# Reordering the hand-over from the first to the second batch of a fused attention and feed-forward kernel

## The chip, the cores and the metric

The kernel runs on one core of a Trainium2 chip. Its time is the device time of one execution in microseconds (us). Engines are called by the names of the profile: PE is TensorE (PEld its weight loads), ACT ScalarE, DVE VectorE, POOL GpSimd, SP SyncE.

## What is computed

```python
# q, k, v: (8, 12, 448, 64) float32: batches, heads, sequence, head size
scores = q @ k.T / sqrt(64) - log(448)
attn   = 1 / (1 + exp(-scores))                 # a sigmoid, no softmax
x      = (attn @ v) -> (8 * 448, 768)           # heads side by side
out    = (max(x @ w_gate, 0) * (x @ w_val)) @ w_out   # 768 -> 1536 -> 768
```

## The kernel before, in words

**Tiles.** A batch has twelve heads, taken in three groups of four (`NG`). The 448 positions of a sequence lie as 64 rows times seven chunks (`NCH`). For scores, keys and queries have to stand with the head dimension on the partitions: a tile `qkT` of a group holds seven chunks of transposed keys and seven of transposed queries. There are three such tiles in turn. Batches 0 and 1 are transposed on TensorE (`pe_transposes`, L195 to L209: up to 14 transposes into one PSUM bank, then one VectorE copy, L206). From batch 2 on, VectorE copies keys and queries into a tile `rel` (L215) and a DMA transpose on the SP queue writes `qkT` (L219).

**Scores and attention.** A score unit (`qk_unit`, L292) is one chunk of keys against all queries of its group: 4 matmuls of 64x64 weights that run side by side, two PSUM banks, and two sigmoid activations of 128x448 on ScalarE (L187). `pv` (L242) sums attention times values over the seven chunks in 28 matmuls and two banks; VectorE scales the sums into `xT` (L184).

**Feed-forward.** `gv` (L304) is one chunk of 128 of the 1536 hidden columns: six matmuls for the gate, six for the value (L309), then max(gate, 0) on ScalarE (L318; on VectorE, L320, for the chunks of batch 0 that are queued with `False`), and the product on VectorE (L327). The chunks stand in `gv_queue`, and `ffn_mix(n)` (L659) takes the next n of it; its hooks are pairs (left, job), and a job is done as soon as no more than `left` chunks are left to do. The projection back to 768 columns follows from batch 2 on, with sums of the weights made by VectorE (`weight_sums`, L403 with L384).

**Batch 0** is handled apart (`FirstSlot`, L263). Its queries are cut in two halves, 256 and 192 columns, so that work can begin with part of them: slots 0 to 2 are the groups with the first half, slots 3 to 5 with the second, each of four score units into two double banks (`pairp`). The table `after` (L691) says what is done behind which unit: transposes, matmuls that keep the clock up, `pv`, and chunks of the feed-forward, which have 256 or 192 columns in this batch.

**Batch 1 and later** (loop at L789). The 21 score units of a batch are cut into six bursts (`cuts`). Behind each burst come `mix[m]` chunks of the batch before; `pv_at` says where within a burst a group's `pv` goes. For batch 1 the hooks put the transposes of groups 1 and 2 (`both`) and the DMA transposes of batch 2 between these chunks.

**Loads.** All loads from L132 on are issued by GpSimd in the order of the program, and convert float32 to float16 on the way. `hold` (L734) is a tiny GpSimd copy out of a `qkT` tile: it keeps GpSimd from issuing the next load before that tile's DMA transpose has landed.

**PSUM** has eight banks. Four are the ring from the start, the other four are batch 0's double banks and join the ring when it is done (L731); each product takes the next bank of the ring.

Of the kernel before, what the change touches and what calls it, by code (L numbers as in the profile page):

```python
# [17 lines left out]
def kernel(  # L18
# [17 lines left out]
    NCH = S // 64  # L36
# [3 lines left out]
    QCUT = 4  # L40
# [40 lines left out]
    def bank16(name):  # L81
        return bank(name, (P, 1024), FP16)
# [20 lines left out]
    def rows_of(src, b):  # L103
        return src[b].rearrange("(x r) (t c) d -> (r t) x (c d)", r=2, c=NCH)

    def load(b, g0, g1, which, c0=0, c1=NCH):
        for nm, t16, src in zip("kq", tiles_of(b), (k, q)):
            if nm in which:
                xs, cs = slice(2 * g0, 2 * g1), slice(c0 * D, c1 * D)
                nc.gpsimd.dma_start(t16[:, xs, cs], rows_of(src, b)[:, xs, cs])  # L110
# [10 lines left out]
    KCUT = 4  # L121
# [22 lines left out]
    def load_gv(f0, f1, which=(0, 1)):  # L144
        fs = slice(f0 * P, f1 * P)
        for i in which:
            wt, src = ((wg, moe_w_gate), (wv, moe_w_val))[i]
            nc.gpsimd.dma_start(wt[:, :, fs], src[:, fs].rearrange("(c p) f -> p c f", p=P))
# [2 lines left out]
    load(0, 1, NG, "q", QCUT)  # L151
    load_gv(0, 2, (1,))
    load_gv(2, 4)
    load_gv(4, 6)
    load(1, 0, 1, "kq")
    load_gv(6, 9)
    load(1, 1, 2, "kq")
    load_v(1)
# [36 lines left out]
    def pe_transposes(b, g, ti, c0=0, c1=NCH):  # L195
        t16 = in_tiles[b][ti]
        qkT = qkT_of(b, g)
        trt = bank16("trt")
        for c in range(c0, c1):
            for h in range(2):  # L200
                nc.tensor.transpose(  # L201
                    trt[64 * h : 64 * h + 64, c * P : (c + 1) * P],
                    t16[:, 2 * g + h, c * D : (c + 1) * D],
                    ident[:],
                )
        nc.vector.tensor_copy(  # L206
            qkT[:, ti * NCH + c0 : ti * NCH + c1, :].rearrange("p c x -> p (c x)"),
            trt[:, c0 * P : c1 * P],
        )  # L209

    def dma_transposes(b, g):
        k16, q16, _ = in_tiles[b]
        rel = relp.tile([P, TW, P], FP16, tag="rel", name="rel")
        for ti, t16 in enumerate((k16, q16)):
            nc.vector.tensor_copy(  # L215
                rel[:, ti * NCH : (ti + 1) * NCH, :].rearrange("p c (h d) -> p h c d", h=2),
                t16[:, 2 * g : 2 * g + 2, :].rearrange("p h (c d) -> p h c d", c=NCH),
            )
        nc.sync.dma_start_transpose(  # L219
            qkT_of(b, g)[:], rel[:].rearrange("p c x -> p (c x)")  # L220
        )
# [433 lines left out]
    def push_first(half, fs, act_relu=True):  # L655
        c0, c1 = HALVES[half]
        push_gv(0, 64 * c0, 64 * (c1 - c0), fs, act_relu)

    def ffn_mix(count, hooks=()):  # L659
        hooks = list(hooks)  # L660
        for left in range(count, -1, -1):
            while hooks and hooks[0][0] >= left:
                hooks.pop(0)[1]()
            if left:
                gv_queue.popleft()()
# [8 lines left out]
    pe_transposes(0, 0, 1, 0, QCUT)  # L674
    keep_warm(2)
    slots = [FirstSlot(half * NG + g, g, half) for half in range(2) for g in range(NG)]
    push_first(0, range(0, 6), False)
    def second_queries():
        for g in range(1, NG):
            pe_transposes(0, g, 1, QCUT, NCH)  # L680

    def pv_then_ffn(i):
        slots[i].pv()
        ffn_mix(1)

    def ffn_then_pv(i):
        ffn_mix(1)
# [3 lines left out]
    after = {  # L691
        (0, 0): lambda: pe_transposes(0, 0, 0, KCUT, NCH),
        (0, 1): lambda: keep_warm(2),
        (0, 2): lambda: pe_transposes(0, 1, 0),
        (0, 3): lambda: pe_transposes(0, 1, 1, 0, QCUT),
        (1, 0): lambda: keep_warm(2),
        (1, 1): lambda: pe_transposes(0, 2, 0),
        (1, 2): lambda: pe_transposes(0, 2, 1, 0, QCUT),
# [7 lines left out]
        (3, 3): lambda: ffn_mix(1),  # L706
        (4, 1): lambda: ffn_then_pv(3),
        (4, 3): lambda: ffn_mix(2),
        (5, 1): lambda: pv_then_ffn(4),
        (5, 3): lambda: ffn_mix(1),  # L710
    }
    for i, slot in enumerate(slots):
        for u in range(4):
# [1 line left out]
            if (i, u) in after:  # L715
                after[(i, u)]()
    slots[5].pv()
    push_first(1, range(0, 6))
    for f0 in range(6, 12, 2):
        for half in range(2):  # L720
            push_first(half, range(f0, f0 + 2))

# [11 lines left out]
    def hold(b, g):  # L734
        nc.gpsimd.tensor_copy(gate[0:1, :], qkT_tiles[(b, g)][0:1, 0, 0:2])

    def both(b, g):
        pe_transposes(b, g, 0)
        pe_transposes(b, g, 1)

    def late_loads():
        dma_transposes(2, 2)
        hold(2, 1)
        load_o()


# [38 lines left out]
            prepare()  # L785
            down(g, i)

    ffn_mix(1, [(1, lambda: both(1, 0))])
    for b in range(1, B):  # L789
        if b == 1:  # L790
            cuts, pv_at = (0, 3, 6, 9, 13, 17, 21), {3: (0, 2), 5: (1, 2)}
        else:
            cuts, pv_at = (0, 4, 7, 11, 14, 18, 21), {0: (-1, 2), 2: (0, 2), 4: (1, 2)}
        bursts = list(range(len(cuts) - 1))
        inner = {}
        if b > 2:
            inner = {0: 1} if b % 2 == 0 else {2: 3, 3: 5} if b == B - 1 else {4: 5}
            for n in inner.values():
                bursts.remove(n)
        count = len(bursts)  # L800
        hooks = {}
        if b == 1:
            mix = (3, 3, 3, 3, 3, 2)
            hooks = {
                1: [(1, lambda: both(1, 1))],
                3: [(1, lambda: both(1, 2))],
                4: [(3, lambda: dma_transposes(2, 0))],
                5: [(2, lambda: dma_transposes(2, 1)), (0, late_loads)],
            }
        elif b == 2:  # L810
            mix = (2, 2, 1, 1, 1, 2)
            hooks = {
                2: [(0, prepare)],
                4: [(0, lambda: weight_sums(0))],
                5: [(1, lambda: weight_sums(1)), (0, lambda: weight_sums(2))],
            }
            open_late()
        elif b == 3:
            mix = (1, 1, 1, 0, 0)
        else:  # L820
            mix = (0,) * count

        def burst(n):
            for i, (g, c) in enumerate(order[cuts[n] : cuts[n + 1]]):
                if n in pv_at and i == pv_at[n][1]:
                    if n == 0:
                        pv_finish(b - 1)
                        if b == 2:
                            push_group(0)
                        elif b % 2 == 0:  # L830
                            push_group(b // 2 - 1)
                    else:
                        pv_group(b, pv_at[n][0])
                qk_unit(b, g, c)

        if b == 3:
            dma_transposes(3, 2)
            for args in put_off:
                stored(*args)
        for m in range(count):  # L840
            jobs = []
            burst(bursts[m])
            if m == 0 and b > 3:
                jobs.append(lambda: dma_transposes(b, 2))
            if b == 2 and m == count - 1:
                jobs.append(lambda: (dma_transposes(3, 0), dma_transposes(3, 1)))
            elif b == 3 and m == count - 1:
                jobs.append(lambda: dma_transposes(4, 1))
            elif 0 <= m - count + 2 and 3 < b < B - 1:
                jobs.append(lambda: dma_transposes(b + 1, m - count + 2))  # L850
            if b == 1:
                if m == 0:
                    load(2, 0, 1, "kq")
                    load(2, 1, 2, "kq")
                    load(2, 2, 3, "kq")
                    load_v(2)
            elif m == 0 and b + 1 < B:
                if b == 3:
                    jobs.append(lambda: hold(3, 2))
                jobs.append(lambda: (load(b + 1, 0, 3, "kq"), load_v(b + 1)))  # L860
            if b % 2 and b > 2:
                if m == count - 1:
                    jobs.append(lambda: (batch_sums_t1(b // 2), batch_sums(b // 2, (0, 1))))
            elif b > 3 and m == 0:
                jobs.append(lambda: batch_sums(b // 2 - 1, (1, HD)))
            if b == 2 and m == count - 1:
                ffn_mix(mix[m], hooks[m])
                next_work(jobs + [lambda: weight_sums(3)], first_act=True)
            elif mix[m]:
                for job in jobs:  # L870
                    job()
                ffn_mix(mix[m], hooks.get(m, ()))
            else:
                next_work(jobs, amid=(lambda: burst(inner[m])) if m in inner else None)
            if b == 3 and m == count - 2:
                dma_transposes(4, 0)
            if b == 3 and m in (1, 3):
                for f in range(*((0, 8, 2), (8, NFC, 2))[m // 2]):
                    gate_sums(f, f + 2)
# [35 lines left out]
```

## Time and profile before

| | us |
|---|---|
| median of 3 runs (lowest, highest) | 392.95 (392.91, 393.34) |
| the profiled execution | 392.75 |
| its span, from first to last instruction | 391.0 |
| PE busy | 384.2 |
| DVE busy | 283.5 |
| ACT busy | 226.9 |

In the lists that follow, a row of a timeline gives the start within the span, how long the row lasts, engine, line, operation, the tile written and those read, the shape and the number of instructions, and in brackets the engine's idle time before it with what ended that. A row of the waits gives who waited for what, the total, how often and the longest. A row of the DMA issues ends with the time from issue to landing. In the row of 40 slices a 9 stands for 90% or more; one slice is 9.8 us. The chain of waits (the work that ended last, in order of time) gives each stretch of matmuls its time up to the next.

### The profile page before, as it was taken

How to read it: one execution, taken by the hardware profiler on the slowest of the kernel's cores; microseconds unless marked ns; L12 is line 12 of the kernel's file. 1: busy time of each engine (PE TensorE's matmuls, PEld its weight loads, DVE VectorE, ACT ScalarE, POOL GpSimd, SP SyncE). 2: the span in 40 equal slices, each digit the busy share in tenths (PEclk: the TensorE clock that was granted, in tenths of full speed). 3: DMA queues.
4: the chain of work that ended last, by engine and by line, in shares of the span. 5: the costliest groups of instructions: out<-in, count | busy, mean ns of one | idle time of the engine just before them, and what ended most of it. 6: DMA issues, size and time to landing. Idle time of an engine off the chain costs nothing.

```text
span 391.0 us, 8760 instructions
## 1 busy us (share of the span) xinstructions
PE 384.2 (98%) x3488; PEld 214.8 (55%) x3488; DVE 283.5 (73%) x557; ACT 226.9 (58%) x480; POOL 49.5 (13%) x73
## 2 busy tenths in 40 slices
PE   8999999999999999999999999999999999999996
PEld 3678786445455545454555554545455555555663
DVE  2454344358387789999757789999987788999663
ACT  5946778784777755555556774545467354333322
POOL 8633420500300300003000300000000000000000
PEclk9999999999999999999999999999999999999999
DMA  9999999998999892225956595132002320000335
GB/s 149 197 199 204 204 204 138 145 202 148 191 185 167 156 217 44 47 49 64 179 99 137 114 222 86 21 49 59 18 14 73 78 80 2 0 1 2 78 87 159
DMA packets 68953, 43.69 MB, mean 112 GB/s; under 512 B 35888, under 2 KB 65584, under 8 KB 68912
## 3 DMA queue, kind: packets, MB, share of 16 engines
q0 software_dynamic: 30736, 23.33, 39.8%
q1 hardware_dynamic: 37664, 19.24, 24.3%
q10 hardware_dynamic: 512, 0.56, 0.5%
q8 instruction: 27, 0.44, 0.5%
q14 instruction: 14, 0.11, 0.1%
HBM read 47.19 MB, written 11.01 MB: 149 GB/s over the span
## 4 chain that ended last, share of the span: by engine, by line
PE 90%; DMA 5%; POOL 1%; DVE 1%; ACT 1%; issue 0%; POOLq 0%; DVEq 0%; ACTq 0%
PE u L393 33%; PE g L393 16%; PE y L393 10%; PE qk_ps L232 8%; PE pv_ps L250 7%; PE g_ps L309 7%; PE v_ps L309 6%; DMA wv<-in_moe_w_val_dram 4%; DMA v<-in_v_dram 2%; PE ya L354 1%; PE trt L201 1%; PE yb L354 1%; POOL k L110 1%; POOL q L110 1%; ACT PT L187 1%
## 5 line engine op out<-in xcount | busy, mean ns | idle before, releaser
L187 ACT ACTIVATE PT<-qk_ps 128x448 f16<-128x448 f32 (+3 forms) x318 | 150.8, 585 | 76.2 <-PE qk_ps L232 76.1
L393 PEld LDWEIGHTS <-S 128*128 128x128 f16 x558 | 54.6, 98 | 44.7
L605 DVE TENSOR_TENSOR gsb<-g,gsb 128x448 f32<-128x448 f32 x72 | 42.8, 625 | 10.3 <-PE g L393 10.0
L232 PE MATMUL qk_ps<-qkT 64*64 64x448 f16 (+2 forms) x756 | 47.4, 335 | 0.8 <-DVE qkT L206 0.5
L327 DVE TENSOR_TENSOR hT<-gate_sb,v_ps 128x256 f16<-128x256 f32 (+2 forms) x36 | 16.2, 465 | 35.2 <-ACT gate_sb L318 18.0
L393 PEld LDWEIGHTS <-hT 128*128 128x128 f16 x306 | 28.7, 98 | 22.3 <-issue 4.9
L601 ACT COPY gsb<-u 128x448 f32<-128x448 f32 x48 | 25.6, 558 | 24.0 <-PE u L393 22.9
L445 ACT ACTIVATE ysb<-u 128x384 f32<-128x384 f32 x31 | 15.2, 491 | 38.2 <-PE u L393 33.8
L250 PE MATMUL pv_ps<-PT,v 64*64 64x448 f16 (+2 forms) x756 | 36.6, 329 | 0.0
L184 DVE TENSOR_SCALAR xT<-pv_ps 128x448 f16<-128x448 f32 (+2 forms) x53 | 27.9, 567 | 11.9 <-PE pv_ps L250 10.8
L309 PE MATMUL v_ps<-xT,wv 128*128 128x256 f16 (+2 forms) x216 | 33.3, 290 | 0.4 <-DMA wv<-in_moe_w_val_dram 0.4
L309 PE MATMUL g_ps<-xT,wg 128*128 128x256 f16 (+2 forms) x216 | 33.5, 291 | 0.1
L393 PEld LDWEIGHTS <-wg 128*128 128x128 f16 x216 | 20.2, 98 | 21.8 <-issue 4.3
L393 PEld LDWEIGHTS <-wv 128*128 128x128 f16 x216 | 21.1, 98 | 19.7
L232 PEld LDWEIGHTS <-qkT 64*64 64x64 f16 x756 | 17.9, 105 | 22.0 <-issue 14.7
L463 DVE SCALAR_TENSOR_TENSOR ysb<-y,ysb 128x384 f32<-128x384 f32 x29 | 16.1, 556 | 17.9 <-PE y L393 10.4
L250 PEld LDWEIGHTS <-v 64*64 64x64 f16 x756 | 21.7, 107 | 10.8 <-issue 0.9
L393 PE MATMUL u<-T,hT 128*128 128x384 f16 x132 | 25.1, 326 | 0.0
L110 POOL DMA_DIRECT2D k<-in_k_dram x14 | 10.9, 776 | 112.4 <-DVE rel L215 105.7
L309 PEld LDWEIGHTS <-wg 128*128 128x128 f16 x216 | 18.5, 98 | 11.7 <-issue 5.1
L309 PEld LDWEIGHTS <-wv 128*128 128x128 f16 x216 | 20.1, 98 | 8.1 <-DMA wv<-in_moe_w_val_dram 0.7
L393 PE MATMUL u<-xT,wg 128*128 128x448 f16 x108 | 23.5, 354 | 0.0
(76 smaller groups left out, 531.2 us busy)
## 6 DMA issues: line engine op xcount, KB each, us to landing
out_dram<-ysb SPq DMA_DIRECT2D x52, 192.0 KB, 2.8
k<-in_k_dram POOLq DMA_DIRECT2D x5, 672.0 KB, 11.4
q<-in_q_dram POOLq DMA_DIRECT2D x5, 672.0 KB, 14.7
v<-in_v_dram POOLq DMA_DIRECT2D x8, 336.0 KB, 14.9
v<-in_v_dram POOLq DMA_DIRECT2D x16, 168.0 KB, 13.8
k<-in_k_dram POOLq DMA_DIRECT2D x8, 224.0 KB, 11.9
wo<-in_moe_w_out_dram POOLq DMA_DIRECT2D x1, 1536.0 KB, 11.1
q<-in_q_dram POOLq DMA_DIRECT2D x6, 224.0 KB, 12.1
```

The source lines that it names most:

```text
L110: nc.gpsimd.dma_start(t16[:, xs, cs], rows_of(src, b)[:, xs, cs])
L184: nc.vector.tensor_scalar(out=xT, in0=src, scalar1=XSCALE, scalar2=None, op0=AOP.mult)
L187: nc.scalar.activation(PT_ap, ps_ap, AF.Sigmoid, bias=sig_bias, scale=qk_scale)
L232: nc.tensor.matmul(out_of(hh)[o : o + 64, :], qkT[rows, c, cols], qkT[rows, NCH + c0 : NCH + c1, cols], start=True, stop=True, tile_positi ...
L250: nc.tensor.matmul(ps[hh][64 * r : 64 * r + 64, 0:qn], v16[rows, 2 * g + hh, c * D : (c + 1) * D], pieces[c][rows, hh, :], start=(c == 0), ...
L309: nc.tensor.matmul(ps[-1][:, 0:qn], wt[:, dc, f * P : (f + 1) * P], xT_tiles[b][:, dc, q0 : q0 + qn], start=(dc == 0), stop=(dc == NDC - 1),)
L327: nc.vector.tensor_tensor(out=hT_tiles[g][:, f, o : o + qn], in0=gate_sb[:, 0:qn], in1=ps[1][:, 0:qn], op=AOP.mult,)
L393: nc.tensor.matmul(ps[:, 0:n], A[:, k_, :], W[:, k_, :], start=(first and k_ == 0), stop=(k_ == kn - 1), skip_group_check=True,)
L445: nc.scalar.activation(o, ps[:, 0:HM], AF.Copy, scale=OUT_SCALE)
L463: nc.vector.scalar_tensor_tensor(out=o, in0=ps[:, 0:HM], scalar=OUT_SCALE, in1=o, op0=AOP.mult, op1=AOP.add)
L601: by(gs[u][i][:], ps[u][:, 0:S])
L605: nc.vector.tensor_tensor(out=gs[u][i][:], in0=ps[u][:, 0:S], in1=gs[u][i][:], op=AOP.add)
```

## The change

Two chunks of batch 0 leave slot 5 and are done among batch 1's bursts; batch 1's first transposes move into slot 5, and its first burst follows directly on batch 0's last `pv`. The keys and queries of batch 1's first group are loaded before, not after, the weights of chunks 4 and 5. In batch 0 the transposes of the second group are split, first four key chunks and four query chunks, then the three other key chunks. For batch 2, the second DMA transpose moves one burst up, the third to behind the first of the last chunks; the load of v moves from behind those of k and q to behind a hold on the third transpose (before, the hold was on the second), ahead of the output weights.

```diff
@@ loads
     load_gv(2, 4)
+    load(1, 0, 1, "kq")
     load_gv(4, 6)
-    load(1, 0, 1, "kq")
     load_gv(6, 9)
@@ batch 0
-    push_first(0, range(0, 6), False)
+    push_first(0, range(0, 4), False)
...
-    def pv_then_ffn(i):
-        slots[i].pv()
-        ffn_mix(1)
+    def first_of_second_group():
+        pe_transposes(0, 1, 0, 0, KCUT)
+        pe_transposes(0, 1, 1, 0, QCUT)
...
-        (0, 2): lambda: pe_transposes(0, 1, 0),
-        (0, 3): lambda: pe_transposes(0, 1, 1, 0, QCUT),
+        (0, 2): first_of_second_group,
+        (0, 3): lambda: pe_transposes(0, 1, 0, KCUT, NCH),
...
-        (5, 1): lambda: pv_then_ffn(4),
-        (5, 3): lambda: ffn_mix(1),
+        (5, 1): slots[4].pv,
+        (5, 2): lambda: (pe_transposes(1, 0, 0), pe_transposes(1, 0, 1)),
...
     slots[5].pv()
-    push_first(1, range(0, 6))
-    for f0 in range(6, 12, 2):
+    push_first(1, range(0, 4))
+    for f0 in range(4, 12, 2):
         for half in range(2):
             push_first(half, range(f0, f0 + 2))
@@ batch 1
     def late_loads():
         dma_transposes(2, 2)
-        hold(2, 1)
+        hold(2, 2)
+        load_v(2)
         load_o()
...
-    ffn_mix(1, [(1, lambda: both(1, 0))])
     for b in range(1, B):
...
         if b == 1:
-            mix = (3, 3, 3, 3, 3, 2)
+            mix = (4, 3, 3, 3, 3, 4)
             hooks = {
                 1: [(1, lambda: both(1, 1))],
                 3: [(1, lambda: both(1, 2))],
-                4: [(3, lambda: dma_transposes(2, 0))],
-                5: [(2, lambda: dma_transposes(2, 1)), (0, late_loads)],
+                4: [(3, lambda: dma_transposes(2, 0)), (1, lambda: dma_transposes(2, 1))],
+                5: [(3, late_loads)],
             }
...
                     load(2, 2, 3, "kq")
-                    load_v(2)
```

## The prediction

> **What bounds the kernel now.** I read the page first, then the list of what TensorE waited for, then its timeline from 0 to 100 us beside those of GpSimd (which issues the loads), ScalarE and VectorE, then the DMA issues one at a time.
>
> ```profile
> PE 384.2 (98%) x3488; PEld 214.8 (55%) x3488; DVE 283.5 (73%) x557; ACT 226.9 (58%) x480; POOL 49.5 (13%) x73
> ...
> PEclk9999999999999999999999999999999999999999
> DMA  9999999998999892225956595132002320000335
> ```
>
> TensorE (PE) is busy for 98% of the span at full granted clock, so a change can save little more than its waits. The DMA row shows a second limit: for about the first 58 us (six slices of 9.8 us) the sixteen DMA engines are full.
>
> ```profile
> PE warm_ps L175 <- DVE zeros L129: 1.2, 1, 1.2
> PE qk_ps L232 <- DVE qkT L206: 0.5, 1, 0.5
> PE v_ps L309 <- DMA wv<-in_moe_w_val_dram: 0.4, 1, 0.4
> PE trt L201 <- DVE k L671: 0.3, 1, 0.3
> ```
>
> These are all the waits of the matmuls. The change can touch the second and the third. Everything else it does must be paid for out of the order of work, and there the loads count. GpSimd's timeline and the DMA issues in two short windows give the times of the keys and queries of batch 1, group 2:
>
> ```profile
> 36.53 0.70 POOL L110 DMA_DIRECT2D k<-in_k_dram  x1 [2.08 <-DMA wv<-in_moe_w_val_dram]
> 37.68 0.71 POOL L110 DMA_DIRECT2D q<-in_q_dram  x1 [0.46 <-DMA k<-in_k_dram]
> ```
>
> ```profile
> k<-in_k_dram POOLq DMA_DIRECT2D x1, 224.0 KB, 12.3
> q<-in_q_dram POOLq DMA_DIRECT2D x1, 224.0 KB, 12.3
> ```
>
> The last figure is us from issue to landing: the keys land at 36.53+12.3 = 48.8 and the queries at 37.68+12.3 = 50.0. TensorE's timeline shows when they are used:
>
> ```profile
> 51.45 0.58 PE L201 MATMUL trt<-ident,k 128*64 128x128 f16 x14
> 51.87 0.56 PE L201 MATMUL trt<-ident,q 128*64 128x128 f16 x14
> 52.35 0.67 PE L309 MATMUL g_ps<-xT,wg 128*128 128x192 f16 x6
> ```
>
> So the transposes of the queries start 1.87 us after the landing (51.87 - 50.0). That is the slack on which my forecast turns.
>
> **The change, part by part.** The number of instructions on each engine stays the same; only their order changes.
>
> *First scores.* The one wait for qkT (0.52 us before 9.94) gets shorter: slot 1 now needs copies of 512 and 512 columns (0.93 us for two) instead of 896 and 512. I estimate 0.3 us. But ScalarE is packed from 10.41 to 19.78 by twelve activations after an idle time of 0.28 us, so at most 0.3 reaches slot 4.
>
> *End of batch 0.* Two feed-forward chunks of 256 columns (f 4 and 5 of the first half) leave slot 5. Back to back such a chunk is g_ps 0.66 + v_ps 0.66 = 1.31 us. The wait for wv (0.45 us before 28.32) goes with them. Changing between 64x64 score matmuls and 128x128 chunks costs about 0.1 us each way in the chain (12 score matmuls 0.69 against 8 without a change 0.38; first g_ps 0.76 against 0.66). Five changes fall away: 0.55 us. ScalarE gives some back: slot 5's four activations (1.51 + 1.19 us) now follow each other, from 26.48 to about 29.2, and the last pv needs the last of them. I get the first burst of batch 1 at 29.35 instead of 33.64 (in the chain of waits); with 2.63 us of chunks put off, and one chunk of 192 columns (0.99) that now stands behind it, that is 33.64 - 2.63 - 0.99 - 29.35 = 0.67 us gained. The keys and queries of group 0 are loaded before the weights 4 to 6 (landing about 24.7 and 25.9 instead of 29.3 and 30.4, at 1.1 us each behind the load at 23.6); they are needed at 27.4, so nothing waits. The weights land 2.2 us later, at 30.4, for use after 34.
>
> *Batch 1 to its last transposes.* TensorE now comes earlier to every load. At group 1 it arrives at 37.5; the keys land at 37.4, the queries at 23.93+14.6 = 38.5, half a microsecond late. At group 2 my count (burst 0.69, four chunks 4.07, burst 0.69, chunks 2.74, transposes with that wait 1.45, chunk 1.09, burst 0.69, chunks 3.73, burst with pv 2.2, chunks 2.07) arrives at about 48.8, exactly at the keys' landing; the queries come at 50.0. The loads cannot come sooner: the same bytes stand ahead of them, each landing follows the last by its size, and the queue never runs empty. So the queries' transposes start at 50.03, 1.84 us earlier than before, while two chunks of 256 columns are still to be done that before lay ahead: 2.63 - 1.84 = **+0.79 us**. All that was gained before this point is swallowed by this wait; were the early part 0.7 us slower, nothing would change.
>
> A rule of the Trainium skill speaks against this. "DMA: Bandwidth & Descriptors", section "Anatomy of one DMA — SWDGE (gpsimd) path", fits a GpSimd load as 2.0 us plus bytes over 436 GB/s. For 224 KB that makes an estimated 0.53 us of transfer where two landings here lie 1.15 us apart; with such loads nothing would be late and the change would end at -0.5. But the page's text does not say which side of a converting copy it counts: HBM read 47.19 MB here for 23.33 MB on the software queue, and by the bytes read the same rule makes 1.05 us. I go by the measured landings.
>
> *Batch 1 after that.* The stretch holds the same parts with two chunks more. One place gets tighter, burst 5. These rows of ScalarE, VectorE and TensorE show it before:
>
> ```profile
> 53.88 3.60 ACT L187 ACTIVATE PT<-qk_ps 128x448 f16<-128x448 f32 x8 [0.48 <-PE qk_ps L232]
> 57.29 0.96 ACT L318 ACTIVATE gate_sb<-g_ps 128x192 f32<-128x192 f32 x3
> ```
>
> ```profile
> 57.73 1.04 DVE L327 TENSOR_TENSOR hT<-gate_sb,v_ps 128x192 f16<-128x192 f32 x3 [3.14 <-ACT gate_sb L318]
> ```
>
> ```profile
> 53.45 0.96 PE L232 MATMUL qk_ps<-qkT 64*64 64x448 f16 x16
> 54.47 0.66 PE L309 MATMUL g_ps<-xT,wg 128*128 128x192 f16 x6
> ...
> 58.17 0.57 PE L232 MATMUL qk_ps<-qkT 64*64 64x448 f16 x8
> 58.57 1.49 PE L250 MATMUL pv_ps<-PT,v 64*64 64x448 f16 x28
> ```
>
> Burst 4 fills eight banks; the chunks behind it can be gated only when eight activations are through (57.29), and the second score unit of burst 5 takes the first chunk's banks. Before, the three chunks were 192, 256, 256 and that chunk's product ended at 58.08, 0.3 ahead. Now they are 256, 192, 192: TensorE gets there 0.33 sooner, the first gate and product take about 0.07 longer each. Shifted to the new time, the product ends at 56.70 and TensorE wants the bank at 56.52: with 0.06 for the semaphore 0.24 lost, and 0.07 more at the pv that follows. I take **+0.3 us** (bounds 0, if the bank is free in time, and 0.5, if VectorE's copies of k and q for the transposes, 0.39 us each, get in front).
>
> *Loads and transposes of batch 2.* v (672 KB) now waits for the third DMA transpose, and the output weights go behind v. Before, the hold released at 67.76. Now the copies for the last transpose are done at 61.7 by my count and a transpose lands 3.9 to 5.8 us after its issue, so 65.9 to 67.6. v adds 3.4 us to the queue (672 KB at the rate of the 224 KB loads); v is used at 82.71 and is there by 75. The second part of the output weights landed at 69.88+14.7 = 84.6 and comes at 85.5 to 87.9; its first use (T, L384) is at 87.61 before, 88.7 now. The next batch's queries landed at 71.69+19.6 = 91.3, now 92.2 to 94.6, for a copy at 94.52 before, 95.6 now. All fit, so I cost this at 0; the cover is 0.8 us in the worst of these, and what is beyond it goes to TensorE one to one, because VectorE is packed from 90.57 to 97.84 and the u at 97.99 waits for its last sum.
>
> **Sum.** 0.79 + 0.3 = +1.1 us. Nothing after 65 us changes in order, and all of it is bound by TensorE, so the shift lasts to the end. The profiled execution took 392.75 us (span 391.0 and 1.75 around it), giving 393.85; the median of the runs shown is 0.2 higher, giving 392.95 + 1.1 = **394.0**.
>
> **Rivals.**
> 1. *The loads are not late* (not slower). The place is the queries' transposes of group 2; it decides from a landing under 49.2 instead of 50.0. For it: the change shortens the early part and puts no byte ahead. Against it: landings in this queue follow each other by size without a gap. Without these two waits the chain is at 48.12 where it was at 51.52, with 2.63 still to do: -0.77, and with the bank wait -0.46: 392.5 (392.2 to 392.5).
> 2. *The wait alone, no bank wait*: +0.5 to +0.79, 393.45 to 393.74. For it: the bank wait rests on margins of 0.2 us.
> 3. *The hold comes late.* If it is released after about 68.6, the queries of batch 3 miss VectorE's copy, and each us more is one at the u near 99. For it: v stands ahead now. Against it: the last transpose has the DMA engines to itself. A release at 70 makes +1.4 more: 395.4.
> 4. *The change doesn't move what it says*: the instruction order shows that it does, so only a late q of group 0 (over 1.5 us) would show here, and 0.7 of that is swallowed.
>
> **How the numbers follow.** A measurement can tell about 0.2% from no change, 0.8 us: below 392.15 is faster, above 393.75 slower. The forecast (393.75 to 394.5) has 0.52, rival 2 0.17, rival 1 0.15, rival 3 0.16. Of rival 1 I give a third to faster, if the early waits are worth more than I count, and of the forecast and rival 3 nearly all to slower: faster 0.06, same 0.27, slower 0.67. The range runs from rival 1's upper half to most of rival 3: 392.4 to 395.2.
>
> **What would show it.** In the new profile: a DMA wait of about 0.5 us at the query transposes near 38 and of 0.7 near 50, the queries landing at 50.0; no wait for wv near 28; the first burst of batch 1 near 29.4; burst 5 near 56.3 with about 0.3 us of lost time; the hold's copy before 68; no new wait of VectorE near 95. I am wrong if the queries of group 2 land before 49.2, or if a wait behind 65 us appears.

## The result, and the profile after

| | before | after |
|---|---|---|
| median, compared on one chip | 393.11 | 393.86 |
| the profiled execution | 392.75 | 393.31 |
| its span | 391.0 | 391.5 |
| first burst of batch 1 / of batch 2 at | 33.57 / 62.46 | 29.41 / 62.91 |

The ratio of the changed kernel to the kernel before is 1.0021, with a 95% interval from 1.0013 to 1.0029: a loss of 0.8 us (0.5 to 1.1). The forecast was a loss of 1.1 us, to 394.0. That 393.86 lies so near 394.0 is in part luck: the forecast started from 392.95, and the kernel before came to 393.11 in this comparison.

The page of the changed kernel has the same limits as before, TensorE and the full DMA engines of the first 58 us:

```profile
PE 384.7 (98%) x3488; PEld 215.8 (55%) x3488; DVE 282.5 (72%) x556; ACT 227.7 (58%) x482; POOL 49.4 (13%) x73
...
DMA  9999995998999893225956596143002320000335
```

All waits of its matmuls (who waited for what, total us, times, longest):

```profile
PE warm_ps L175 <- DVE zeros L129: 1.2, 1, 1.2
PE qk_ps L232 <- ACT PT L187: 0.6, 2, 0.3
PE trt L201 <- DMA q<-in_q_dram: 0.5, 1, 0.5
PE pv_ps L250 <- ACT PT L187: 0.2, 1, 0.2
```

The waits for qkT, for wv and for k (L671) are gone. In their place are short waits for ScalarE (0.33 us before 9.81, 0.23 before 27.20, 0.16 before 29.33), where score matmuls now follow each other closely, and one for a load: the queries of batch 1, group 2. Their DMA issue at 37.05 (the last figure is us from issue to landing):

```profile
q<-in_q_dram POOLq DMA_DIRECT2D x1, 224.0 KB, 12.3
```

They land at 49.34, and TensorE's timeline shows the transposes behind them:

```profile
48.28 0.58 PE L201 MATMUL trt<-ident,k 128*64 128x128 f16 x14
49.38 0.58 PE L201 MATMUL trt<-ident,q 128*64 128x128 f16 x14 [0.52 <-DMA q<-in_q_dram]
```

TensorE stands idle for 0.52 us behind the keys' transposes; the queries' begin 0.04 behind the landing. Before, TensorE came 1.89 us after it (51.87 against 49.98). The second place is burst 5 of batch 1, on TensorE:

```profile
55.71 0.79 PE L232 MATMUL qk_ps<-qkT 64*64 64x448 f16 x8
56.13 1.77 PE L250 MATMUL pv_ps<-PT,v 64*64 64x448 f16 x28
57.55 0.72 PE L232 MATMUL qk_ps<-qkT 64*64 64x448 f16 x8
58.21 0.50 PE L309 MATMUL g_ps<-xT,wg 128*128 128x256 f16 x3
```

From the first score matmul to the first chunk it takes 2.50 us (58.21 - 55.71); before it took 2.21 (60.38 - 58.17), as these rows of TensorE before show, with the row at 58.17 in the prediction:

```profile
59.90 0.55 PE L232 MATMUL qk_ps<-qkT 64*64 64x448 f16 x8
60.38 0.67 PE L309 MATMUL g_ps<-xT,wg 128*128 128x192 f16 x6
```

The same eight score matmuls last 0.79 and 0.72 instead of 0.57 and 0.55. No wait is listed, since each pause is short and lies between matmuls of one row; it is read from the lengths. What they pause for is the products of the chunks before, whose banks they need. VectorE's timeline, cut at 55.9, has the first one:

```profile
55.64 0.42 DVE L327 TENSOR_TENSOR hT<-gate_sb,v_ps 128x256 f16<-128x256 f32 x1 [3.13 <-ACT gate_sb L318]
```

It ends at 56.06. The second score unit, which had begun at 55.93, goes on at 56.12, and the trace names this product as what released it. The second product ends at 56.33, and a `pv` matmul that it released starts at 56.38.

The balance of this execution: the queries' transposes start 2.49 us sooner than before (49.38 against 51.87), 2.63 us of chunks are still to do: +0.14. Burst 5: +0.29. Together +0.43, and the first burst of batch 2 stands 0.45 later (62.91 against 62.46). From there to the end the two timelines keep that distance to 0.1 us, and the span is 0.5 longer.

So the mechanism is the forecast's, with a smaller amount. It is smaller because the queries landed at 49.34 here, 0.64 sooner than in the profile of before (49.98). Whether that is the change's doing or the chance of one execution is asked below, by e2 and e5 above all.

### The profile page after: what moved, and what is told of

It is laid out like the page before. It is cut to its first block, busy times and chain, and to the rows that moved or that the text cites. A ratio compares the mean times of both kernels' runs of the same rounds, so it can differ in the third digit from the quotient of the medians.

```text
span 391.5 us, 8756 instructions
## 1 busy us (share of the span) xinstructions
PE 384.7 (98%) x3488; PEld 215.8 (55%) x3488; DVE 282.5 (72%) x556; ACT 227.7 (58%) x482; POOL 49.4 (13%) x73
## 4 chain that ended last, share of the span: by engine, by line
PE 85%; DMA 10%; POOL 2%; DVE 1%; issue 1%; ACT 0%; POOLq 0%; DVEq 0%; ACTq 0%
PE u L393 33%; PE g L393 16%; PE y L393 10%; PE qk_ps L232 7%; PE pv_ps L250 6%; PE g_ps L309 5%; PE v_ps L309 5%; DMA k<-in_k_dram 4%; DMA q<-in_q_dram 3%; DMA wg<-in_moe_w_gate_dram 3%; PE ya L354 1%; POOL q L110 1%; PE yb L354 1%; POOL k L110 1%; ACT PT L187 0%
## 5 line engine op out<-in xcount | busy, mean ns | idle before, releaser
L327 DVE TENSOR_TENSOR hT<-gate_sb,v_ps 128x256 f16<-128x256 f32 (+2 forms) x36 | 16.2, 465 | 36.6 <-ACT gate_sb L318 18.5
L463 DVE SCALAR_TENSOR_TENSOR ysb<-y,ysb 128x384 f32<-128x384 f32 x29 | 16.1, 556 | 17.9 <-PE y L393 10.4
```

The lines of the kernel that those rows point to most:

```text
L327: nc.vector.tensor_tensor(out=hT_tiles[g][:, f, o : o + qn], in0=gate_sb[:, 0:qn], in1=ps[1][:, 0:qn], op=AOP.mult,)
L463: nc.vector.scalar_tensor_tensor(out=o, in0=ps[:, 0:HM], scalar=OUT_SCALE, in1=o, op0=AOP.mult, op1=AOP.add)
```

## The experiments

Theory: from 50 us on the changed kernel is bound by the landing of group 2's queries, one to one, and it loses 0.3 more at burst 5. Rivals: the loss has another place (the order of batch 2's loads, the loads of a later batch), or slack behind the wait takes it up. Each time is a median and stands beside the median of the kernel before on the same chip; the ratio and its interval go by all executions and need not equal the quotient of the two medians. Expected texts that name "the changed kernel's profile" mean the one above.

**The keys and queries first (e1).** They are loaded ahead of the last weights, on which nothing near 50 us depends.

```diff
+    load(1, 2, 3, "kq")
     load_gv(9, 12)
-    load(1, 2, 3, "kq")
```

> The changed kernel with one swap: the keys and queries of batch 1, group 2, are loaded ahead of the weights of chunks 9 to 11 instead of behind them. My theory (the changed kernel waits for these queries): they land near 44, the transposes run from 48.3 to 49.2 without the wait of 0.5, and all behind them comes 0.7 us earlier; the wait for the weights 9 to 11 stays hidden, since they land near 49.4 for a chunk that starts near 51.6. Time 0.7 to 1.0 us under the changed kernel, so about 392.9 to 393.2. Rival (the loss sits in burst 5 or in the late loads): the transposes may come earlier, but the time stays within 0.2 us of the changed kernel, 393.9.

Measured: 393.30 against 392.89, ratio 1.0014 (1.0006 to 1.0023). The queries land at 43.63, and their transposes follow the keys' at 48.78 without a wait. The first burst of batch 2 comes at 62.28, 0.18 sooner than before: in this profile the place decides, as the theory has it. But the time misses the expected 392.9 to 393.2, and the interval overlaps that of the changed kernel (1.0013 to 1.0029), so the medians alone don't show a gain. In this execution the gain does not last. At 120.61 TensorE waits 0.45 us for a sum of VectorE, which had waited for the queries of batch 4 (VectorE's timeline):

```profile
117.70 0.39 DVE L215 COPY rel<-q 128x896 f16<-128x896 f16 x1 [1.04 <-DMA q<-in_q_dram]
```

In the profiles of before and after these queries are there 0.06 to 0.07 us ahead of that copy (landing at 116.72 for 116.79, and 117.15 for 117.21); in e1 they land at 117.67.

**One chunk more in front of burst 5 (e2).** The chunks between the bursts are shared out anew, so that the banks of burst 5 are wanted one chunk later.

```diff
-            mix = (4, 3, 3, 3, 3, 4)
+            mix = (4, 3, 3, 3, 4, 3)
...
-                4: [(3, ...dma_transposes(2, 0)), (1, ...dma_transposes(2, 1))],
-                5: [(3, late_loads)],
+                4: [(4, ...dma_transposes(2, 0)), (2, ...dma_transposes(2, 1))],
+                5: [(2, late_loads)],
```

> The changed kernel with four chunks behind burst 4 and three behind burst 5 instead of three and four, the jobs between them at the same chunk. My theory (burst 5 waits for banks, 0.24 us in the changed kernel's profile): burst 5 comes one chunk (0.99 us) later, finds its banks free, and its stretch from the first score to the next chunk takes 2.21 us as before the change instead of 2.50. Time 0.3 us under the changed kernel, 393.55. Rival (the whole loss is the wait for the queries): time unchanged, 393.85.

Measured: 393.89 against 392.89, ratio 1.0031 (1.0019 to 1.0044). Burst 5 takes 2.21 us again (57.83 to 60.04): the 0.29 is the wait for the banks, and it goes. The expected 393.55 was missed all the same. In the profiled execution the loads were later, on TensorE's timeline:

```profile
50.19 0.58 PE L201 MATMUL trt<-ident,q 128*64 128x128 f16 x14 [1.04 <-DMA q<-in_q_dram]
```

Landing at 50.15: 0.81 later than in the first profile of the changed kernel, with not one byte more in front of it. So e2 shows the place of the 0.29, and its medians leave open what it is worth in time. What it shows besides is that the landing varies from execution to execution.

**Both (e3).**

> The two edits together: group 2's keys and queries loaded ahead of the last weights, and four and three chunks behind bursts 4 and 5. My theory: the two waits are on the path one after the other, so the gains add up to 1.0 to 1.3 us: 392.55 to 392.85, 0.3 to 0.5 under the kernel before. Rival (they hide one another, or the early gain is lost again further on): not under 393.1.

Measured: 393.24 against 392.89, ratio 1.0007 (0.9997 to 1.0018): with both waits taken away no loss is left that can be measured, but the expected 0.3 to 0.5 under the kernel before did not come. In its profile TensorE has no wait at the transposes of group 2, but comes to them 0.63 later than in e1 (49.00 against 48.37), as its first burst of batch 1 is late already (30.13 against 29.44), and the first burst of batch 2 is at 62.63. Some is lost later: 0.31 at 76.7, because the last part of v of batch 2 lands only at 75.49 (its hold came later by one chunk), and 0.3 more near 121 by batch 4's queries (a wait of 0.71 of VectorE).

**The late part undone (e4).** The loads of batch 2 stand as in the kernel before, the rest is the changed kernel.

```diff
-        hold(2, 2)
-        load_v(2)
+        hold(2, 1)
...
                     load(2, 2, 3, "kq")
+                    load_v(2)
```

> The changed kernel with the late loads as before the change: v of batch 2 issued with k and q, the hold on the second transpose. My theory (the hold and v cost nothing, everything behind them lands in time): the same time as the changed kernel within 0.2 us, 393.65 to 394.05. Rival (v ahead of the output weights delays VectorE and so TensorE): 0.3 us or more under the changed kernel.

Measured: 394.88 against 392.89, ratio 1.0055 (1.0038 to 1.0072), worse than the changed kernel, where the same time was expected. So the late part is no part of the loss; in this kernel it saves something. The DMA issues show what, here for the first DMA transpose (at 53.4, landing 63.7):

```profile
qkT<-rel SPq DMA_TRANSPOSE x1, 10.4
```

and the same issue in the changed kernel, where v is not in the queue beside it:

```profile
qkT<-rel SPq DMA_TRANSPOSE x1, 6.7
```

With v's 672 KB still coming in, the transpose takes some 3.6 us longer. VectorE's timeline shows who pays: its copies for the third transpose need the `rel` tile that the first one reads.

```profile
63.85 0.39 DVE L215 COPY rel<-k 128x896 f16<-128x896 f16 x1 [2.38 <-DMA qkT<-rel]
```

Behind that copy stands a product (L327), and TensorE waits 0.59 us for it at 64.93. The kernel with the late part undone is 1.23 us behind before at 61.6 and 2.34 at 67.0.

**The changed kernel again (e5).** No edit.

> The changed kernel once more, unaltered, for the spread of the landing. My theory (TensorE is released by the landing of group 2's queries, so the time follows the landing): its profile shows the queries' transposes within 0.1 us behind the landing, and the first burst of batch 2 at 62.9 plus the landing's distance from 49.34; time 0.5 to 1.0 us over the kernel before. Rival (the loss is of a fixed size and elsewhere): the burst's place does not follow the landing.

Measured: 393.71 against 393.16, ratio 1.0024 (1.0013 to 1.0034). Its profile has the late landing (50.15), on TensorE's timeline:

```profile
50.20 0.58 PE L201 MATMUL trt<-ident,q 128*64 128x128 f16 x14 [0.58 <-DMA q<-in_q_dram]
```

The balance: 51.87 - 50.20 = 1.67, so 2.63 - 1.67 = +0.96; burst 5 +0.29; together +1.25. The first burst of batch 2 is at 63.73, +1.27, and the span 392.3, +1.3. The forecast had 0.79 + 0.3 for a landing at 49.98. Between the two profiled executions of the changed kernel the landing differs by 0.81 us (49.34, 50.15) and the time by 0.81 (393.31, 394.12).

**Batch 4's loads by groups (e6, e7).** After e1 a rival was that batch 4's late queries cost the changed kernel something in the executions that aren't profiled. e6 is the changed kernel, e7 the kernel before, each with the first group's keys and queries of batch 4 loaded first.

```diff
-    load(b + 1, 0, 3, "kq")
+    if b == 3: load(4, 0, 1, "kq"), load(4, 1, 3, "kq")
+    else: load(b + 1, 0, 3, "kq")
```

> The changed kernel with batch 4's keys and queries loaded as group 0 first, then groups 1 and 2, in place of all groups at once. In the changed kernel's profile VectorE's copy of these queries starts 0.06 us behind their landing at 117.15. My theory: this second meeting with a load costs the changed kernel only where its loads run slow, so 0 to 0.3 us off, 393.5 to 393.9, and a narrower spread. Rival (it is the bulk of the loss): 0.5 us or more off.

> The kernel before with the same edit to batch 4's loads. There the copy starts 0.07 us behind the landing at 116.72. Theory: as for the changed kernel, 0 to 0.3 us off, 392.6 to 392.95. If this gains as much as the same edit to the changed kernel, batch 4's loads have no part in the difference between the two.

Measured: e6 393.97 against 393.16, ratio 1.0027 (1.0016 to 1.0038); e7 393.04, ratio 0.9999 (0.9989 to 1.0009). Neither gains; batch 4 is not where the loss is. e6 has the landing at 50.09 and the first burst of batch 2 at 63.66. e7 shows something about the kernel *before*: its loads ran 0.36 us ahead of the first profile (queries at 49.62), its wait for wv was gone, and the first burst of batch 2 came 0.36 sooner, at 62.10. So the kernel before moves with its loads too, through the wait for wv, which is listed as 0.45; e10 below shows that it is worth up to 0.61.

**All mends together (e8).** e3, with the third transpose and the hold on it one chunk earlier again, and e6.

> The changed kernel with the queries of group 2 loaded ahead of the last weights, four and three chunks behind bursts 4 and 5, the third DMA transpose of batch 2 ahead of the last three chunks, and batch 4's loads by group. Theory: no wait for group 2's queries, no wait for banks in burst 5, v of batch 2 there before its first use at 75, no wait for batch 4's queries: the first burst of batch 2 at 62.0 against 62.46 in the kernel before, and all of that kept: 0.4 to 0.6 us under the kernel before, 392.3 to 392.5. Rival (the early gain is lost to another meeting with the loads): not under the kernel before by more than 0.2 us.

Measured: 393.11 against 393.16, ratio 0.9999 (0.9990 to 1.0008). The interval lies below the changed kernel's (1.0013 to 1.0029), so the loss is gone. That points to the mends at the two places, since batch 4's loads gained nothing in e6 and e3 has no measurable loss without them. But the expected 392.3 to 392.5 was missed. The profile is what was hoped for (transposes without a wait at 48.40 and 48.81, burst 5 in 2.21, first burst of batch 2 at 62.03, 0.43 sooner, span 390.7), but the median equals that of the kernel before. In e7, and in e10 and e11 below, the kernel before stands at 62.03 to 62.10 as well, as soon as its loads come 0.3 to 0.5 sooner. Measured against these, the mended hand-over is worth nothing. Why it isn't ahead in the medians either, where executions with late loads count too, stays open.

**More load in front of the queries (e9, e12).** Two loads of 224 KB, and one, ahead of group 2's keys and queries.

```diff
     load_gv(9, 12)
+    for i, src in enumerate((k, q)):          # e12: k alone
+        nc.gpsimd.dma_start(wo[:, 2*i : 2*i + 2, 0 : NCH*D], rows_of(src, 1)[:, 4:6, :])
     load(1, 2, 3, "kq")
```

> The changed kernel with two more loads of 224 KB each ahead of the keys and queries of batch 1, group 2 (into a part of the output weights' tile that is overwritten later; the output is the same). Theory: TensorE waits for these queries, and from there on it is bound one to one by their landing: 2 x 1.15 = 2.3 us later, 52.4 instead of 50.1, transposes behind it at 52.45, first burst of batch 2 near 66.0, and the time 2.3 us over that of the changed kernel (393.7 in the comparisons so far), 396.0, ratio to the kernel before 1.007 to 1.008. Rival (the landing is late, but slack behind it takes most of that up, so that the loss comes from the order of work and not from the wait): less than 1 us over the changed kernel, ratio under 1.005.

> The changed kernel with one more load of 224 KB ahead of the keys and queries of batch 1, group 2 (into a part of the output weights' tile that is overwritten later; the output is the same). Theory: the queries land 1.13 us later than in the changed kernel (49.3 to 50.15 there, so 50.5 to 51.3 here), TensorE's two waits in front of the transposes make 1.2 to 2.0 us in all, the clock stays whole behind them (with two such loads the waits made 2.5 us and the granted clock was 0.50 for 3 us), and the time is 1.1 us over the changed kernel: 394.8 to 395.0, ratio 1.0050. Rival 1 (slack behind the wait takes it up): less than 0.5 us over the changed kernel, ratio under 1.0035. Rival 2 (the shorter wait lowers the clock, too): a granted clock of about 0.5 for some us behind 51, and 1.2 us more, ratio about 1.008.

Measured, e12: 394.98 against 392.84, ratio 1.0054 (1.0042 to 1.0066). TensorE's timeline:

```profile
49.74 0.58 PE L202 MATMUL trt<-ident,k 128*64 128x128 f16 x14 [1.52 <-DMA k<-in_k_dram]
50.69 0.58 PE L202 MATMUL trt<-ident,q 128*64 128x128 f16 x14 [0.37 <-DMA q<-in_q_dram]
```

The queries land at 50.65, 1.31 after those of the changed kernel's first profile; the first burst of batch 2 is at 64.22, 1.31 later, and the span is 1.3 longer. One to one; no slack behind the wait takes anything up.

e9: 397.0 against 393.1, ratio 1.0102 (1.0085 to 1.0118): 1.0 us over the expected 396.0. The queries land at 52.16 (2.82 later: 2.23 by the two loads, 0.59 because all loads before them were later). The keys' transposes wait 1.99 us, the queries' 0.52. And then, by stretches of 1 us of TensorE (busy, granted clock, DMA share, GB/s):

```profile
52.20:53.20 1.00, 1.00 (x19) 0.98 1.27 203
53.20:54.20 1.00, 1.00 (x7) 0.50 1.26 203
54.20:55.20 1.00, 1.00 (x9) 0.50 1.26 202
55.20:56.20 1.00, 1.00 (x16) 0.50 1.28 206
56.20:57.20 1.00, 1.00 (x14) 0.81 1.15 184
```

The clock is halved for some 3.4 us (0.02 + 3 x 0.50 + 0.19 = 1.71 us missing, at half speed), from 53.17 on, a microsecond after the second wait. From the queries' transposes to burst 5 it takes 7.82 us (52.20 to 60.02) instead of 6.33 (49.38 to 55.71), 1.49 more; since TensorE is slower there, the banks of burst 5 are free in time, and the 0.29 goes. 2.82 + 1.49 - 0.29 = 4.02, and the first burst of batch 2 stands 4.02 later (66.93 against 62.91). One of the five executions seems to show the case without the slow clock: its mean granted clock is 1.000 where the others have 0.994 to 0.996, and it took 395.85 us, near the expected 396.0.

**Parts of the change by themselves (e10, e11).** The kernel before with the split of the second group's transposes alone, and with the late part alone (the three DMA transposes, the hold, v and the output weights).

```diff
# e10
-        (0, 2): lambda: pe_transposes(0, 1, 0),
-        (0, 3): lambda: pe_transposes(0, 1, 1, 0, QCUT),
+        (0, 2): lambda: (pe_transposes(0, 1, 0, 0, KCUT), pe_transposes(0, 1, 1, 0, QCUT)),
+        (0, 3): lambda: pe_transposes(0, 1, 0, KCUT, NCH),
# e11
-        hold(2, 1)
+        hold(2, 2)
+        load_v(2)
...
-                4: [(3, ...dma_transposes(2, 0))],
-                5: [(2, ...dma_transposes(2, 1)), (0, late_loads)],
+                4: [(3, ...dma_transposes(2, 0)), (1, ...dma_transposes(2, 1))],
+                5: [(1, late_loads)],
```

> The kernel before with one part of the change alone: the transposes of batch 0's second group are split. Theory (the prediction's first step): the wait for qkT falls from 0.52 to about 0.3, at most 0.3 reaches slot 4, and the wait for wv near 28 takes it up, since those weights land when they did: ratio 0.999 to 1.000, the first burst of batch 2 within 0.2 us of 62.46. Rival (the split gains by itself and lasts): 0.3 us less, ratio 0.9992, and the first burst of batch 2 at 62.2 or sooner.

> The kernel before with the late part alone: the second DMA transpose of batch 2 one burst earlier, the third behind the first of the last chunks, v of batch 2 behind a hold on the third, the output weights behind v. Theory (what this part saves in the changed kernel it saves only because there the first DMA transpose is used sooner): the first DMA transpose lands 2 us or more sooner than at 62.1, but TensorE's first burst of batch 2 at 62.46 did not wait for it, and nothing behind waits for v or the output weights: ratio 0.9995 to 1.0005. Rival 1 (the late part gains by itself): ratio 0.9985 or less. Rival 2 (the hold comes late for the loads behind it, as the prediction's third rival has it): a wait of VectorE for the queries of batch 3 near 94 and a loss of 0.5 us or more, ratio over 1.001.

Measured, e10: 392.78 against 393.10, ratio 0.9997 (0.9987 to 1.0006). The split gains 0.28 at slot 1 (9.66 against 9.94). In this profile the lead lasts up to the first chunk's gate (18.76 against 19.05) and is gone at its value (19.70 against 19.72): the value weights of that chunk land at 19.66, so a load takes the gain up here too, only sooner than expected. The wait for wv behind 27 is gone for another reason, early loads: wv is there at 27.64, and the matmuls start at 27.71 instead of 28.32, 0.61 sooner. At 62 some of that goes: the first DMA transpose lands at 62.01, 0.04 ahead of the first burst of batch 2 (62.05), so it is the limit there.

e11: 393.31 against 393.10, ratio 1.0006 (0.9996 to 1.0017), no loss and no gain that can be measured. The first DMA transpose lands at 59.03 instead of 62.06, and in the profile of before nobody had waited for it. In this profile the 0.43 gained by early loads is lost again at 99, on TensorE's timeline:

```profile
99.09 0.57 PE L232 MATMUL qk_ps<-qkT 64*64 64x448 f16 x8 [0.40 <-DMA qkT<-rel]
```

That transpose of batch 3 was issued at 94.54 and landed 4.5 us later; in the kernel before it was issued at 94.97, landed at 99.08, and was wanted at 99.12. A lead of 0.4 us can thus be lost to a late landing further on, here at this transpose and in e1 at batch 4's queries. It need not be: in e7, e8 and e10 the same transpose is issued as early (94.52 to 94.59), takes 4.1 us, and nobody waits for it.

## Why the prediction was right, and where it was not

**The step that decided was right:** the queries' landing, the chunks still to do, and one to one to the end. In the profiles of the changed kernel's load order the transposes start 0.04 to 0.05 behind the landing (49.34 and 50.15 in the changed kernel, 50.15, 50.11 and 50.09 in e2, e4 and e6), e12 moves the landing by 1.31 and the whole rest by 1.31, and e1 takes the wait away by moving two loads.

**Its size was given for one landing.** The forecast says "the queries come at 50.0" and "+0.79". The landings of that load order ran from 49.34 to 50.15, in kernels that had the same bytes in front, so the term is 0.14 to 0.96. The measured loss of 0.8 us is below the sum of 1.1, though its interval (0.5 to 1.1) reaches it. The profiles show how it can be less: the kernel before moves with its loads, too, through its wait for wv, which I took for a fixed one, but not as far. With early loads in both, the first burst of batch 2 is at 62.91 in the changed kernel and at 62.03 to 62.10 in the kernel before (e7, e10, e11), 0.8 to 0.9 us apart. How often each landing occurs outside the profiled executions isn't known.

**Burst 5** was right: 0.29 for 0.3, released by the products, as forecast, and gone when one chunk more stands in front of it (e2, e8).

**Batch 0's end** was right: first burst of batch 1 at 29.41 where "near 29.4" was forecast, no wait for wv. In e3 and e5 that burst came at 30.13 and 30.11; as forecast, the wait for group 2's queries swallowed such a difference in e5. One statement ahead of the sum was not quite right: the number of instructions per engine did change (ScalarE 480 to 482, VectorE 557 to 556), since the two chunks that moved take their gates on ScalarE now.

**The wait near 38** failed: "the keys land at 37.4, the queries [...] at 38.5, half a microsecond late". In the first profile the queries landed at 37.87 and were used at 38.00 without a wait; with later loads (e2, e6) the wait is 0.18 and 0.26. It wouldn't have mattered, since the next wait takes it up.

**The late part at 0** was right for the changed kernel, but with two errors. "v is used at 82.71" names batch 2's second `pv`: the first one was at 75.06 in the profile of before, so v, landing at 73.70 for 75.50, has 1.8 us of cover and not eight; e3, with its hold one chunk later, lost 0.31 there. And I priced only what this part could cost, not what it avoids: without it the change loses some 1.2 us more (e4's span is 393.5, e5's with the queries as late 392.3), since the DMA transpose then takes 10.4 us beside v's load.

**Rival 1** (loads not late) priced the chain at 48.12 without waits and the time at 392.5. It did not come about by itself. Where the loads were moved to make it so (e1, e8), the keys' transposes began at 48.37 and 48.40 (48.44 and 48.47 in the chain of waits), so the lead was overstated by 0.3; and the time was 393.1 to 393.3. In e1 what was left of the lead was lost again at the queries of batch 4; in e8 a lead of 0.43 is no lead over a kernel before whose loads are early. **Rival 2** (no bank wait) is refuted by the 0.29 and by e2. **Rival 3** (hold late) did not happen in the changed kernel: the hold's copy at 65.67, no wait of VectorE near 95. **Rival 4** fell with the profile: everything moved as described.

## What to carry to other kernels

When work is moved from ahead of a load's use to behind it, the use can come sooner, but the load doesn't. So first count, at each load that follows, how long it lies ready before it is used. The smallest of these reserves is the most that can be gained up to there; as the moved work still has to be done later, what it takes beyond that reserve turns into a loss. Before trusting a reserve of a microsecond, look at the landing in more than one profile: here it varied by 0.8 us with the same bytes in front.

## What the runs showed of the hardware that I had not expected

- **The clock falls after a short wait.** In e9's profile waits of 1.99 and 0.52 us, with 0.6 us of transposes between them, were followed by a granted clock of one half for about 3.4 us, which cost 1.49 us of matmul time; one of the five executions of e9 seems to have kept its clock (a mean of 1.000, 395.85 us). In e12 waits of 1.52 and 0.37 us left it whole. The Trainium skill, "TensorE: Matmul & The Clock Gate", section "Part 1: The HAM clock gate", has the clock halved after at least one idle window of about 3.4 us and whole again after about 3.4 us of work. The time to recover agrees with this run. The wait did not need to be 3.4 us long here; the measurement decides.
- **A DMA transpose suffers from loads beside it.** 10.4 us from issue to landing with v's load in the queues (e4), 6.7 us with only the rest of the k and q loads (the changed kernel), 4.0 us for the next one, which had the engines nearly to itself (57.01 to 60.98). With the order of the kernel before it was 8.0 us with v's load (e10) and 4.8 without (e11).
- **The same load lands up to 0.8 us apart** from execution to execution (49.34 to 50.15), and a kernel that waits for it shows it in full (393.31 and 394.12 us).
